# Left output projection with products of 512 columns instead of 256, its even and odd heads summed apart and added by three engines

## The chip, the cores and the metric

The kernel runs on one core of a Trainium2 chip. The metric is the device time of one execution in microseconds (us); a median of several runs is given where there are several. Engines are named as in the profile: PE (TensorE, matmuls), PEld (its weight loads), DVE (VectorE), ACT (ScalarE), POOL (GpSimd) and SP (SyncE, here the queue that streams weights).

## The reference

The input x has 2048 rows of 1024. It is normalised by rows to xn. Part A goes over 64 segments of 32 rows, with a memory of 8 rows that is carried from one segment to the next:

```python
for s in range(n_seg):                      # 64 segments, seg_len 32, M = 8, 32 heads of 128
    h = jnp.concatenate([mem, xs], axis=1)  # 40 rows
    q, k, v = (jnp.einsum('btd,dhe->bhte', h, W) for W in (Wq, Wk, Wv))
    scores = jnp.einsum('bhqe,bhke->bhqk', q, k) * scale
    p = _softmax(jnp.where(mask[None, None], scores, -1000000000.0), axis=-1)
    o = jnp.einsum('bhqk,bhke->bhqe', p, v)
    o = jnp.einsum('bhte,hed->btd', o, Wo)
    mem = o[:, :M, :].copy()
    outs.append(o[:, M:, :])
```

Part B routes: the two rows of xn with the largest product with w_r go through a gated MLP (1024 to 3584 and back), times the sigmoid of that product, and are added to xn there. The output is x + A(xn) + B(xn), in bfloat16.

## The kernel before

**Main rows and left rows.** The first output rows of a segment become the next segment's memory, so the segments run one after another. Of a segment's 32 rows of x, the first 24 (XM) are worked on together with the 8 rows of memory: 32 "main" rows. Its last 8 rows, the "left" rows, depend on no output for their projections, and four segments' left rows are worked on together as one tile of 32 rows. Four segments make a group G; j is the place of a segment in its group (s = 4 G + j). Their attention still needs the segment's keys, so it runs with the segment; its result goes to OTL (32 heads, 4 segments, 8 rows).

**Weights.** The weights of Q, K, V and the output are cut into 64 granules of 128 x 2048. 44 stay in SBUF; 20 are streamed again in each segment by SP through five slots, tile `g`, `fetch()` at L350 (one granule and three quarters of another are kept in PSUM). Granules 48 to 63 are the output's, two heads each.

**Order in a segment.** Six phases p = 0 to 5 (halves of Q, K, V as in `PHASES`), each of eight granules kc: at L785 four products of 32 rows by 512 columns, in four column groups of PE, into `PSm`. At a phase's end ACT copies PSm to SBUF (XB at L804, VM at L814), and PE turns it three granules into the next phase (L621). Scores are formed at (2,6) and (4,6) (L644, L646), DVE and ACT do the softmax (exponential L663, sums L668, last reader of the scores L687), `attend` forms the heads' outputs (L707, L709; copies L716, L718). Phase 6 is the output: 16 granules, each with eight products of 256 columns at L571 (`project`) into `WO`, which DVE adds to the rows of x (L854). The norm and the turns for the next segment run in between.

**Left passes.** The left rows' projections of a group are spread over other segments as passes on granules that are in SBUF at that time. The table `PASSES` names for each unit the place (j, phase, kc) and the granules. The units of Q, K and V run `left_pass` (L564, four products of 512); the unit "o", the output of the previous group's left rows, runs `project` (L571, eight products of 256, from OTL) into `WL`, ten granules at the end of the segment j = 3 and six in the next segment, j = 0. At the place in `COPIES` the unit is copied out: for "o", one addition by DVE (L593) of WL to OL, the left rows of x after `sum_left`, and four stores by POOL (L596). OL is loaded by `load_left` in the segment j = 3. In the last segment all 16 passes "o" follow the main ones.

**Release.** A slot of `g` is loaded anew when PE's last product on it, main or left, has run. After the last segment the routed rows' MLP runs, with its weights loaded into places that have come free.

Of the kernel before, what the change touches and what calls it, by code (L numbers as in the profile page):

```python
# [8 lines left out]
BF16 = mybir.dt.bfloat16  # L9
F32 = mybir.dt.float32  # L10
U32 = mybir.dt.uint32
ALU = mybir.AluOpType
# [31 lines left out]
}  # L44

COPIES = {"q0": (1, 1, 0, "scalar"), "q1": (1, 5, 7, "vector"), "k0": (2, 2, 0, "scalar"), "k1": (3, 1, 0, "scalar"),
          "v0": (3, 4, 7, "scalar"), "v1": (3, 5, 7, "scalar"), "o": (0, 4, 3, "vector")}


@with_exitstack  # L50
def kernel(
# [16 lines left out]
    nc = tc.nc  # L68
    P = 128
    Bsz, S, D = A_x.shape  # L70
    H, E = A_Wq.shape[1], A_Wq.shape[2]
    M = A_mem0.shape[1]
    SEG = int(A_seg_len)
# [9 lines left out]
    XM = SEG - M  # L83
# [34 lines left out]
    one = ctx.enter_context(tc.tile_pool(name="one", bufs=1, reuse_waits="tile"))  # L118
# [78 lines left out]
    for s in range(4):  # L197
        nc.vector.tensor_copy(out=SELM[:, s, :, 0:XM],
                              in_=IDENT[:, 32 * s:32 * s + XM].unsqueeze(1).to_broadcast([P, 4, XM]))
        nc.vector.tensor_copy(out=SELL[:, s, :, :],  # L200
                              in_=IDENT.rearrange("p (s c) -> p s c", c=32)[:, :, XM:SEG])
# [103 lines left out]
    def new_stl(PTl):  # L305
        stl = one.tile([P, KC, SEG], BF16, tag="stl", name="STL")
        nc.scalar.copy(out=gview(stl), in_=PTl[:, :, :, :])
        return stl
# [2 lines left out]
        PTm = turn(OB)  # L311
        nc.vector.tensor_copy(out=gview(st)[:, :, :, XM:SEG], in_=PTm[:, :, :, XM:SEG])

    def load_left(G, t):
        o4 = x2[4 * G * SEG:4 * (G + 1) * SEG, :].rearrange("(s r) d -> s r d", s=4)
        for g in range(4):
            nc.gpsimd.dma_start(out=t[32 * g:32 * (g + 1), :], in_=o4[:, XM:SEG, 256 * g:256 * (g + 1)])
        return t

    def norm_left(t, G):  # L320
# [87 lines left out]
    def granule(g):  # L408
        if g in res_tiles:
            return res_tiles[g]  # L410
        got, t = queued.pop(0)
        assert got == g, (got, g)
        return t
# [107 lines left out]
    def group_of(u, s):  # L521
        G, j = divmod(s, 4)
        if u == "o":
            return G if j == 3 else G - 1
        return G + 1
# [22 lines left out]
    def begin(u):  # L548
        PS = psL.tile([P, 512], F32, tag="accl", name="WL" if u == "o" else "PSl")
        units[u] = [PS, 16 if u == "o" else 8]  # L550

    def one_pass(u, g, Gv):
        if u not in units:
            begin(u)
        PS, n = units[u]
        units[u][1] = n - 1
        if u == "o":
            project(PS, g - 48, Gv, lhs_left, n == 1, first=(n == 16))
        else:
            left_pass(PS, g, Gv, n == 8, n == 1)  # L560

    def left_pass(PSl, g, Gv, first_, last_):
        for jq in range(4):
            nc.tensor.matmul(PSl[32 * jq:32 * jq + 32, :], lhsT=STL[:, g % KC, :], rhs=part(Gv, jq),  # L564
                             start=first_, stop=last_, tile_position=(0, 32 * jq))

    def project(PS, w, Gv, lhs, last, first=False):
        for hs in range(2):
            h = 2 * w + hs
            for g in range(4):  # L570
                nc.tensor.matmul(PS[32 * g:32 * g + 32, 0:256], lhsT=lhs(h),  # L571
                                 rhs=Gv[:, D * hs + 256 * g:D * hs + 256 * (g + 1)], start=(first and hs == 0),
                                 stop=(last and hs == 1), tile_position=(0, 32 * g), skip_group_check=True)

    def lhs_left(h):
        return otl_of[0][:, h, :, :].rearrange("p s r -> p (s r)")

    xl_of, otl_of = [None], [None]

    def copy_unit(u, s, engine):  # L580
        PS, n = units.pop(u)
        assert n == 0, (u, s, n)
        Gu = group_of(u, s)
        copy = nc.scalar.copy if engine == "scalar" else nc.vector.tensor_copy
        half = int(u[-1]) if u != "o" else 0
        if u[0] == "v":
            new_vl[half] = one.tile([P, 512], BF16, tag=roles[half], name="VL")
            copy(out=new_vl[half][:, :], in_=PS[:, :])
            if half:
                roles.insert(0, roles.pop())  # L590
        elif u == "o":
            OL = xl_of[0]
            nc.vector.tensor_tensor(out=OL[:, :], in0=PS[:, 0:256], in1=OL[:, :], op=ALU.add)  # L593
            o4 = out2[4 * Gu * SEG:4 * (Gu + 1) * SEG, :].rearrange("(s r) d -> s r d", s=4)
            for g in range(4):
                nc.gpsimd.dma_start(out=o4[:, XM:SEG, 256 * g:256 * (g + 1)], in_=OL[32 * g:32 * (g + 1), :])  # L596
        else:
            XBl = one.tile([P, 512], BF16, tag=roles[0], name="XBl")
            copy(out=XBl[:, :], in_=PS[:, :])
            stores.append(lambda: nc.scalar.dma_start(out=ql_d[Gu][2 * half + "qk".index(u[0])], in_=XBl[:, :]))  # L600
            if engine == "scalar":
                stores.pop()()

    for s in range(NSEG):
        G, j = divmod(s, 4)
# [89 lines left out]
        def attend(half, ph, turn_too=None):  # L695
            if half not in sums:
                if half not in OT:
                    OT[half] = one.tile([P, 4, 4, SEG], BF16, tag=("kt", "bC")[half], name="OT")
                if half == 0:
                    nxt["wo"] = psA.tile([P, 512], F32, tag="acc", name="WO")  # L700
                sums[half] = [BS[:, 0:4 * NK] if half else nxt["wo"][:, 256:256 + 4 * NK], OPB]
            PTm, PTl = PTs[half]
            for il in range(4):
                for jl in range(2):
                    q0 = 32 * (2 * ph + jl)
                    o = sums[half][jl][:, il * NK:(il + 1) * NK]
                    nc.tensor.matmul(o, lhsT=VM[half][q0:q0 + 32, il * P:(il + 1) * P], rhs=PTm[q0:q0 + 32, il, 0:NK],  # L707
                                     start=True, stop=False, tile_position=(q0, 0), skip_group_check=True)
                    nc.tensor.matmul(o, lhsT=VL[half][q0:q0 + 32, il * P:(il + 1) * P], rhs=PTl[q0:q0 + 32, il, 0:NK],  # L709
                                     start=False, stop=True, tile_position=(q0, 0), skip_group_check=True)  # L710
            if turn_too is not None:
                turn_too()
            for jl in range(2):
                ov = sums[half][jl].rearrange("p (i q) -> p i q", i=4)
                copy = nc.scalar.copy if half == 0 or jl == 0 else nc.vector.tensor_copy
                copy(out=OT[half][:, 2 * ph + jl, :, :], in_=ov[:, :, 0:SEG])  # L716
                h0 = 16 * half + 8 * ph + 4 * jl
                copy(out=left_out()[:, h0:h0 + 4, j, :], in_=ov[:, :, SEG:NK])  # L718
# [58 lines left out]
        for p, (mat, half) in enumerate(PHASES):  # L777
# [3 lines left out]
            for kc in range(KC):  # L781
                g = 8 * p + kc
                Gv = back if s > 0 and g == KEPT_WHOLE else granule(g)
                for jq in range(4):
                    nc.tensor.matmul(PSm[32 * jq:32 * jq + 32, :], lhsT=ST[:, kc, :], rhs=part(Gv, jq),  # L785
                                     start=(kc == 0), stop=(kc == KC - 1), tile_position=(0, 32 * jq))
# [45 lines left out]
        for w in range(16):  # L832
            if w == 5:
                attend(1, 0)
            if w == 8 and s + 1 < NSEG:
                attend(1, 1, lambda: turned.append(turn(xn, BS[:, 160:288].bitcast(BF16))))
                nxt["st"] = new_st(turned[0])
            elif w == 8:
                attend(1, 1)
            if w == 12 and left_too is not None:  # L840
                STL = new_stl(turn(left_too))
            Gv = granule(48 + w)
            project(WO, w, Gv, lhs_main, w == 15, first=(w == 0))
            held[48 + w] = Gv
            run_passes(6, w)
            if w == 9 and s + 1 < NSEG:
                new_lx(s + 1)
                bring_back(1, nc.scalar.copy)
                bring_back(2, nc.vector.tensor_copy)
            if w == 11 and j == 3:  # L850
                xl_of[0] = load_left(G, one.tile([P, 256], BF16, tag="stl", name="OL")[:, :])
            release(6, w)
        OB = X[s % 2]
        nc.vector.tensor_tensor(out=OB[:, :], in0=WO[:, 0:256], in1=OB[:, :], op=ALU.add)  # L854
# [66 lines left out]
    for w in range(2):  # L921
        for kc in range(KC):
            for fh in range(2):
                Gt = moe_tiles["gu", w, kc, fh]
                for fl in range(FC // 2):
                    col = (w * FC + fh * (FC // 2) + fl) * 2
                    nc.tensor.matmul(GU[:, col:col + 2], lhsT=Gt[:, fl * P:(fl + 1) * P], rhs=XSELT[:, kc, :],
                                     start=(w + kc + fh + fl == 0), stop=True, skip_group_check=True)
# [6 lines left out]
    for fg in range(FC // 2):  # L935
        Gt = moe_tiles["dn", fg]
        for a in range(2):
            fc = 2 * fg + a
            for g in range(4):
                nc.tensor.matmul(YP[32 * g:32 * g + 2, 0:256], lhsT=HT[:, fc, :],  # L940
                                 rhs=Gt[:, a * D + 256 * g:a * D + 256 * (g + 1)], start=(fc == 0), stop=(fc == FC - 1),
                                 tile_position=(0, 32 * g))
# [39 lines left out]
```

## Time and profile before

| | |
|---|---|
| median of 3 runs | 1893.31 us (1886.54 to 1896.8) |
| the profiled execution: time, span | 1904.66 us, 1903.0 us |
| mean granted clock of TensorE | 0.955 |
| DMA | 704.02 MB, 370 GB/s in the mean |
| PE matmuls, loads | 36008, 36008 |
| left output products: from resident, from streamed granules | 1408, 640 (128x256) |
| additions at L593 | 16, 390 ns each |

All rows of the prediction come from the profiled execution. In the groups of instructions the columns are: line, engine, operation, output<-input, shape, count, then busy us and mean ns of one, then the idle us of the engine before them and what ended them. "issue" is idle time that ended with nothing that the profile shows. The tables of waits read: who waited for whom, us in total, times, longest.

### The profile page before, as it was taken

What the parts mean: (1) busy time and instruction counts of PE and PEld (TensorE: products, weight loads), DVE (VectorE), ACT (ScalarE), POOL (GpSimd) and SP (SyncE); (2) the same over time, 40 slices, a digit from 0 to 9 for tenths busy, and PEclk for the clock granted to TensorE, in tenths of its full rate; (3) what the DMA queues carried; (4) which work ended last, traced back from release to release, by engine and by line L of the source; (5) the groups of instructions that cost most, each with busy time, mean ns of one, the idle gap of its engine ahead of it and who ended that gap; (6) DMA issues with size and microseconds to landing.
All of it is one profiled execution on the core that took longest, in us unless ns stands there. A gap on an engine that the chain in (4) does not pass through costs nothing.

```text
span 1903.0 us, 82489 instructions
## 1 busy us (share of the span) xinstructions
PE 1583.4 (83%) x36008; PEld 884.0 (46%) x36008; DVE 898.3 (47%) x2970; ACT 683.9 (36%) x1923; POOL 441.6 (23%) x882
## 2 busy tenths in 40 slices
PE   3558888888888988898888988888898898888764
PEld 1224545445454545444454544445444454545443
DVE  5825544544445444544455444544444454445430
ACT  1113433343334433343333333334333343333320
POOL 3211222213131322213121322213132221312220
PEclk9669999999999999999999999999999999999995
DMA  9999999999999999999999999999999999999998
GB/s 359 406 345 377 368 376 371 369 363 367 385 370 380 376 373 375 389 364 352 376 364 379 376 380 367 354 383 361 354 343 379 368 371 377 373 379 352 373 393 330
DMA packets 232090, 704.02 MB, mean 370 GB/s; under 512 B 39296, under 2 KB 61232, under 8 KB 231728
## 3 DMA queue, kind: packets, MB, share of 16 engines
q1 hardware_dynamic: 194384, 662.92, 92.5%
q0 software_dynamic: 28704, 27.96, 4.7%
q10 hardware_dynamic: 8640, 7.87, 1.2%
q8 instruction: 282, 4.62, 0.9%
q14 instruction: 80, 0.66, 0.1%
HBM read 685.93 MB, written 22.16 MB: 372 GB/s over the span
## 4 chain that ended last, share of the span: by engine, by line
DMA 53%; PE 42%; issue 3%; ACT 1%; DVE 1%; SPq 1%; POOL 0%; ACTq 0%; POOLq 0%; DVEq 0%
DMA g<-wsc 45%; PE PSm L785 22%; PE WO L571 6%; PE PSl L564 5%; PE BT L621 3%; PE WL L571 3%; DMA g<-in_A_Wv_dram 1%; DMA MW<-in_B_w_gate_dram 1%; DMA MW<-in_B_w_up_dram 1%; DMA g<-in_A_Wq_dram 1%; PE BS L644 1%; DMA wres<-in_A_Wv_dram 1%; DMA g<-in_A_Wk_dram 1%; DMA wres<-in_A_Wo_dram 1%; DMA g<-in_B_w_down_dram 1%
## 5 line engine op out<-in xcount | busy, mean ns | idle before, releaser
L785 PE MATMUL PSm<-wres,ST 128*32 128x512 bf16 x8448 | 707.7, 385 | 19.6 <-DMA wres<-in_A_Wv_dram 8.3
L785 PEld LDWEIGHTS <-ST 128*32 128x32 bf16 x12288 | 325.7, 96 | 418.5 <-issue 199.9
L785 PE MATMUL PSm<-g,ST 128*32 128x512 bf16 x3588 | 363.8, 388 | 105.7 <-DMA g<-wsc 75.3
L571 PEld LDWEIGHTS <-OT 128*32 128x32 bf16 x8192 | 221.7, 98 | 162.4 <-issue 143.1
L571 PE MATMUL WO<-wres,OT 128*32 128x256 bf16 x5632 | 243.5, 280 | 25.6 <-issue 18.6
L804 ACT CAST XB<-PSm 128x512 bf16<-128x512 f32 x256 | 150.0, 586 | 311.2 <-PE PSm L785 307.8
L480 POOL DMA_DIRECT2D LX<-ql_d x63 | 33.6, 533 | 826.2 <-PE WO L571 399.4
L571 PE MATMUL WO<-g,OT 128*32 128x256 bf16 x2560 | 135.9, 284 | 78.8 <-DMA g<-wsc 67.1
L564 PE MATMUL PSl<-wres,STL 128*32 128x512 bf16 x2112 | 187.4, 395 | 0.8 <-issue 0.7
L856 POOL DMA_DIRECT2D out_dram<-X x256 | 129.4, 513 | 217.3 <-DVE X L854 179.5
L273 POOL DMA_DIRECT2D X<-in_A_x_dram x256 | 129.8, 511 | 183.2 <-PE PSm L785 77.3
L377 DVE COPY g<-BT 128x512 bf16<-128x512 bf16 x63 | 26.7, 425 | 294.4 <-ACT QT L629 224.1
L373 ACT COPY BK<-KEPT 128x512 bf16<-128x512 bf16 x126 | 75.8, 602 | 133.4 <-PE WO L571 133.4
L854 DVE TENSOR_TENSOR X<-WO,X 128x256 bf16<-128x256 f32 x64 | 27.2, 425 | 195.5 <-PE WO L571 195.5
L564 PEld LDWEIGHTS <-STL 128*32 128x32 bf16 x3072 | 85.7, 99 | 59.4 <-issue 14.6
L629 ACT COPY QT<-BT 128x512 bf16<-128x512 bf16 x128 | 74.9, 585 | 106.1 <-PE BT L621 100.8
L621 PEld LDWEIGHTS <-XB 128*128 128x128 bf16 x1024 | 58.7, 98 | 105.8 <-ACT XB L804 58.7
L814 ACT CAST VM<-PSm 128x512 bf16<-128x512 f32 x128 | 75.8, 592 | 85.1 <-PE PSm L785 83.4
L707 PEld LDWEIGHTS <-VM 32*128 32x128 bf16 x2048 | 65.6, 91 | 83.9 <-issue 68.5
L621 PE MATMUL BT<-IDENT,XB 128*128 128x128 bf16 x1024 | 102.6, 223 | 2.3 <-ACT QKL L499 1.4
L653 DVE TENSOR_TENSOR BS<-BS,CT 128x96 f32<-128x96 f32 (+1 forms) x256 | 59.6, 233 | 85.6 <-PE BS L646 81.2
L716 ACT CAST OT<-BS 128x128 bf16<-128x128 f32 x128 | 34.0, 265 | 178.5 <-PE BT L709 85.2
(173 smaller groups left out, 2425.6 us busy)
## 6 DMA issues: line engine op xcount, KB each, us to landing
g<-wsc SPq DMA_DIRECT2D x1134, 512.0 KB, 6.1
LX<-ql_d POOLq DMA_DIRECT2D x63, 128.0 KB, 6.0
g<-wsc SPq DMA_DIRECT2D x63, 128.0 KB, 5.0
ql_d<-XBl ACTq DMA_DIRECT2D x60, 128.0 KB, 5.6
MW<-in_B_w_gate_dram SPq DMA_DIRECT2D x16, 448.0 KB, 9.3
MW<-in_B_w_up_dram SPq DMA_DIRECT2D x16, 448.0 KB, 9.0
wres<-in_A_Wk_dram SPq DMA_DIRECT2D x12, 512.0 KB, 11.8
MW<-in_B_w_down_dram SPq DMA_DIRECT2D x12, 512.0 KB, 10.2
```

The source lines that it names most:

```text
L273: nc.gpsimd.dma_start(out=X[s % 2][32 * g:32 * g + XM, :], in_=x2[s * SEG:s * SEG + XM, 256 * g:256 * (g + 1)])
L373: copy(out=back[c][:, :], in_=KEPT_COLS[KEPT_WHOLE][c])
L564: nc.tensor.matmul(PSl[32 * jq:32 * jq + 32, :], lhsT=STL[:, g % KC, :], rhs=part(Gv, jq), start=first_, stop=last_, tile_position=(0, 32 ...
L571: nc.tensor.matmul(PS[32 * g:32 * g + 32, 0:256], lhsT=lhs(h), rhs=Gv[:, D * hs + 256 * g:D * hs + 256 * (g + 1)], start=(first and hs == ...
L621: nc.tensor.transpose(out=PTq[:, il, :, :].rearrange("p j r -> p (j r)"), in_=XB[:, il * P:(il + 1) * P], identity=IDENT[:, :])
L629: nc.scalar.copy(out=QT[half][:, :, :], in_=pv)
L653: nc.vector.tensor_tensor(out=S4, in0=S4, in1=m, op=ALU.add)
L707: nc.tensor.matmul(o, lhsT=VM[half][q0:q0 + 32, il * P:(il + 1) * P], rhs=PTm[q0:q0 + 32, il, 0:NK], start=True, stop=False, tile_position ...
L785: nc.tensor.matmul(PSm[32 * jq:32 * jq + 32, :], lhsT=ST[:, kc, :], rhs=part(Gv, jq), start=(kc == 0), stop=(kc == KC - 1), tile_position= ...
L804: nc.scalar.copy(out=XB[:, :], in_=PSm[:, :])
L814: nc.scalar.copy(out=VM[half][:, :], in_=PSm[:, :])
L856: nc.gpsimd.dma_start(out=out2[s * SEG:s * SEG + XM, 256 * g:256 * (g + 1)], in_=OB[32 * g:32 * g + XM, :])
```

## The change

A left output pass now has four products of 512 columns: an even head's into rows 0 to 63 of WL (one half of the columns in rows 0 to 31, the other in rows 32 to 63), an odd head's into rows 64 to 127. The sum over the heads thus stands in two places, 64 rows apart, and is put together at the end: ACT copies half of each across the rows to a new tile LF (which takes the buffer of OTL), DVE adds the other half, POOL adds LF to OL. The column blocks of OL lie in another order ("crossed"), in its loads and its stores. The six passes of j = 0 and the sum stand at other places of the segment.

```diff
-          (3, 8, 0): [52, 54], (0, 1, 5): [55], (0, 2, 2): [57], (0, 2, 5): [58], (0, 3, 2): [60], (0, 3, 5): [61],
-          (0, 4, 2): [63]},
+          (3, 8, 0): [52, 54], (0, 0, 7): [55], (0, 1, 3): [57], (0, 1, 7): [58], (0, 2, 3): [60], (0, 2, 6): [61],
+          (0, 3, 2): [63]},
...
-          "v0": (3, 4, 7, "scalar"), "v1": (3, 5, 7, "scalar"), "o": (0, 4, 3, "vector")}
+          "v0": (3, 4, 7, "scalar"), "v1": (3, 5, 7, "scalar"), "o": (0, 3, 3, "vector")}
...
+            b = 2 * (g % 2) + g // 2 if crossed else g
+            nc.gpsimd.dma_start(out=t[32 * g:32 * (g + 1), :], in_=o4[:, XM:SEG, 256 * b:256 * (b + 1)])
...
-            project(PS, g - 48, Gv, lhs_left, n == 1, first=(n == 16))
+            project_left(PS, g - 48, Gv, n == 16, n == 1)
...
+    def project_left(PS, w, Gv, first, last):
+
+        for hs in range(2):
+            lhsT = otl_of[0][:, 2 * w + hs, :, :].rearrange("p s r -> p (s r)")
+            for c in range(2):
+                r0 = 64 * hs + 32 * c
+                nc.tensor.matmul(PS[r0:r0 + 32, :], lhsT=lhsT, rhs=Gv[:, D * hs + 512 * c:D * hs + 512 * (c + 1)],
+                                 start=first, stop=last, tile_position=(0, r0))
...
-            nc.vector.tensor_tensor(out=OL[:, :], in0=PS[:, 0:256], in1=OL[:, :], op=ALU.add)
+            LF = one.tile([P, 256], F32, tag="otl", name="LF")
+            for c in range(2):
+                nc.scalar.copy(out=LF[64 * c:64 * c + 64, :], in_=PS[64 - 64 * c:128 - 64 * c, 256 * c:256 * c + 256])
+            for c in range(2):
+                here = slice(64 * c, 64 * c + 64)
+                nc.vector.tensor_tensor(out=LF[here, :], in0=PS[here, 256 * c:256 * c + 256], in1=LF[here, :], op=ALU.add)
+            nc.gpsimd.tensor_tensor(out=OL[:, :], in0=LF[:, :], in1=OL[:, :], op=ALU.add)
...
+                b = 2 * (g % 2) + g // 2
+                nc.gpsimd.dma_start(out=o4[:, XM:SEG, 256 * b:256 * (b + 1)], in_=OL[32 * g:32 * (g + 1), :])
```

In what the engines are given, three places show it. Before, PE has the pass on granule 55 in phase 1 of a segment j = 0, between granules 13 and 14 (wres_298 is granule 14, wres_1137 granule 55), eight pairs of a load and a product of 256:

```order
L785 LDWEIGHTS ST
L785 MATMUL PSm<-g,ST 32x512
L571 LDWEIGHTS OTL
L571 MATMUL WL<-wres_1137,OTL 32x256
...
L785 LDWEIGHTS ST
L785 MATMUL PSm<-wres_298,ST 32x512
```

Now it stands at the end of phase 0, between granules 7 and 8 (wres_228 and wres_232), as four pairs with 512 columns:

```order
L799 LDWEIGHTS ST
L799 MATMUL PSm<-wres_228,ST 32x512
L584 LDWEIGHTS OTL
L584 MATMUL WL<-wres_1137,OTL 32x512
...
L799 LDWEIGHTS ST
L799 MATMUL PSm<-wres_232,ST 32x512
```

The whole list of PE has 2048 rows fewer. On ACT, phases 2 to 4 of a segment j = 0, before:

```order
L804 CAST XB<-PSm 128x512
L629 COPY QT<-BT 128x512
L663 ACTIVATE BS<-BS 128x320
L804 CAST XB<-PSm 128x512
L634 COPY KT<-QKL 128x16x8
L636 COPY KT<-BT 128x16x32
```

and now:

```order
L818 CAST XB<-PSm 128x512
L643 COPY QT<-BT 128x512
L602 COPY LF<-WL 64x256 x2
L677 ACTIVATE BS<-BS 128x320
L818 CAST XB<-PSm 128x512
L648 COPY KT<-QKL 128x16x8
L650 COPY KT<-BT 128x16x32
```

The two copies to LF stand ahead of the exponential and of the copy XB of phase 3. On DVE at the same place, before:

```order
L659 TENSOR_TENSOR BS<-BS,NM 128x320
L668 TENSOR_REDUCE DN<-BS 128x8
L669 RECIPROCAL DN<-DN 128x8
L675 TENSOR_TENSOR PT_12472<-BS,DN 128x256
L687 TENSOR_TENSOR BX<-BS,DN 128x8x8
L689 STREAM_TRANSPOSE PT_12472<-PT_12472 128x256
L691 STREAM_TRANSPOSE PT_12472<-BX 128x256
L593 TENSOR_TENSOR OL<-WL,OL 128x256
L653 TENSOR_TENSOR BS<-BS,CT 128x4x24
```

and now:

```order
L673 TENSOR_TENSOR BS<-BS,NM 128x320
L605 TENSOR_TENSOR LF<-WL,LF 64x256 x2
L682 TENSOR_REDUCE DN<-BS 128x8
L683 RECIPROCAL DN<-DN 128x8
L689 TENSOR_TENSOR PT_12257<-BS,DN 128x256
L701 TENSOR_TENSOR BX<-BS,DN 128x8x8
L703 STREAM_TRANSPOSE PT_12257<-PT_12257 128x256
L705 STREAM_TRANSPOSE PT_12257<-BX 128x256
L667 TENSOR_TENSOR BS<-BS,CT 128x4x24
```

The addition behind the softmax of the first half has become two, ahead of its sums.

More of the change, by code (lines that the diff above doesn't have):

```diff
@@ L312, in mem_to_st, with load_left @@
         nc.vector.tensor_copy(out=gview(st)[:, :, :, XM:SEG], in_=PTm[:, :, :, XM:SEG])
-    def load_left(G, t):
+    def load_left(G, t, crossed=False):
         o4 = x2[4 * G * SEG:4 * (G + 1) * SEG, :].rearrange("(s r) d -> s r d", s=4)
         for g in range(4):
-            nc.gpsimd.dma_start(out=t[32 * g:32 * (g + 1), :], in_=o4[:, XM:SEG, 256 * g:256 * (g + 1)])
+            b = 2 * (g % 2) + g // 2 if crossed else g
+            nc.gpsimd.dma_start(out=t[32 * g:32 * (g + 1), :], in_=o4[:, XM:SEG, 256 * b:256 * (b + 1)])
         return t
@@ L573, in project @@
                                  stop=(last and hs == 1), tile_position=(0, 32 * g), skip_group_check=True)
-    def lhs_left(h):
-        return otl_of[0][:, h, :, :].rearrange("p s r -> p (s r)")
     xl_of, otl_of = [None], [None]
+    def project_left(PS, w, Gv, first, last):
[5 more added lines that the diff above has]
+                                 start=first, stop=last, tile_position=(0, r0))
     def copy_unit(u, s, engine):
@@ L592, in copy_unit @@
             OL = xl_of[0]
-            nc.vector.tensor_tensor(out=OL[:, :], in0=PS[:, 0:256], in1=OL[:, :], op=ALU.add)
+            LF = one.tile([P, 256], F32, tag="otl", name="LF")
[5 more added lines that the diff above has]
+            nc.gpsimd.tensor_tensor(out=OL[:, :], in0=LF[:, :], in1=OL[:, :], op=ALU.add)
             o4 = out2[4 * Gu * SEG:4 * (Gu + 1) * SEG, :].rearrange("(s r) d -> s r d", s=4)
             for g in range(4):
-                nc.gpsimd.dma_start(out=o4[:, XM:SEG, 256 * g:256 * (g + 1)], in_=OL[32 * g:32 * (g + 1), :])
+                b = 2 * (g % 2) + g // 2
+                nc.gpsimd.dma_start(out=o4[:, XM:SEG, 256 * b:256 * (b + 1)], in_=OL[32 * g:32 * (g + 1), :])
         else:
@@ L850 @@
             if w == 11 and j == 3:
-                xl_of[0] = load_left(G, one.tile([P, 256], BF16, tag="stl", name="OL")[:, :])
+                xl_of[0] = load_left(G, one.tile([P, 256], BF16, tag="stl", name="OL")[:, :], True)
             release(6, w)
```

## The prediction

> **What bounds the kernel now.** I read the page's totals and its chain first, then the table of waits for PE and for the DMA queue, then PE's timeline around the left products, last the segments one against another.
>
> ```profile
> PE 1583.4 (83%) x36008; PEld 884.0 (46%) x36008; DVE 898.3 (47%) x2970; ACT 683.9 (36%) x1923; POOL 441.6 (23%) x882
> q8 instruction: 282, 4.62, 0.9%
> DMA 53%; PE 42%; issue 3%; ACT 1%; DVE 1%; SPq 1%; POOL 0%; ACTq 0%; POOLq 0%; DVEq 0%
> ...
> SPq L350 <- PE PSm L785: 475.2, 651, 5.7
> SPq L350 <- PE WL L571: 59.9, 63, 2.8
> ...
> PE PSm L785 <- DMA g<-wsc: 75.3, 158, 1.7
> PE WO L571 <- DMA g<-wsc: 67.1, 132, 2.1
> PE WO L571 <- issue: 20.8, 21, 2.1
> PE WL L571 <- issue: 11.5, 8, 2.3
> PE PSm L785 <- issue: 9.2, 10, 2.5
> ```
>
> Two things take turns. The weight stream makes PE wait (75.3 + 67.1 us), and the stream itself waits for PE to free one of its five slots (475.2 us behind PSm, 59.9 us behind WL). So a loss on PE is not simply hidden: the ring is often full, and then the transfers stand still with PE. The three last rows are such losses: 20.8 + 11.5 + 9.2 = 41.5 us in 39 waits in which PE waited for no engine and no transfer. One of them, in PE's timeline (start, length, line, count, idle time before):
>
> ```profile
> 1518.16 0.39 PE L571 MATMUL WO<-wres,OT 128*32 128x256 bf16 x8
> 1518.38 0.61 PE L571 MATMUL WL<-wres,OTL 128*32 128x256 bf16 x16
> 1521.33 0.40 PE L571 MATMUL WL<-wres,OTL 128*32 128x256 bf16 x8 [2.34 <-issue]
> ```
>
> PE stops for 2.34 us between two left passes whose operands have long been there. What it lacks is instructions. Row q8 says so first: 282 packets carry 4.62 MB, 16.4 KB each, and PE with its weight loads has 36008 + 36008 = 72016 instructions, so one packet is 255 of them. Second, the count between two such stops: this is every matmul that started between the stop that ended at 1515.12 us and this one (groups of PE in that window, of four rows with x4 the last is shown).
>
> ```profile
> L571 PE MATMUL WO<-wres,OT 128*32 128x256 bf16 x46 | 2.0, 273 | 0.5 <-issue 0.5
> L571 PE MATMUL WO<-g,OT 128*32 128x256 bf16 x24 | 1.2, 274 | 0.0
> L571 PE MATMUL WL<-g,OTL 128*32 128x256 bf16 x24 | 1.2, 273 | 0.0
> L571 PE MATMUL WL<-wres,OTL 128*32 128x256 bf16 x16 | 0.6, 273 | 0.0
> ...
> L709 PE MATMUL BT<-PT,VL 32*128 32x40 bf16 x4 | 0.3, 174 | 0.0
> L293 PE MATMUL BS<-IDENT,XN 128*128 128x128 bf16 x2 | 0.3, 224 | 0.0
> ```
>
> 46 + 24 + 24 + 16 + 4 x 4 + 2 = 128 matmuls, with their loads 256 instructions: the stops lie one block apart. A block that is used up faster than the next one arrives makes PE stop. A pass of 256 columns uses 16 instructions in the time in which a pass of 512 uses 8:
>
> ```profile
> 978.50 0.39 PE L785 MATMUL PSm<-g,ST 128*32 128x512 bf16 x4
> 978.71 0.39 PE L571 MATMUL WL<-wres,OTL 128*32 128x256 bf16 x8
> 978.93 0.82 PE L785 MATMUL PSm<-wres,ST 128*32 128x512 bf16 x12
> ```
>
> From start to start, four products of 512 take 0.21 us and eight of 256 take 0.22 us. What a stop costs is seen in the first segments of the groups (j = 0): seven begin with a stop among the first passes or just behind them, eight don't. The windows' columns are length, then busy time of the engines, clock, DMA share and GB/s; first and last of the seven with their sum, then of the eight.
>
> ```profile
> 431.76:460.13 28.37, 23.20 (x568) 13.57 (x560) 13.80 (x49) 10.57 (x30) 9.91 (x19) 1.00 1.01 371
> 1518.61:1547.55 28.94, 24.02 (x570) 14.54 (x562) 13.70 (x49) 10.44 (x30) 10.34 (x20) 0.94 1.00 367
> sum 202.25, PE 168.91 PEld 98.62 DVE 96.48 ACT 73.43 POOL 70.94; mean PE 24.13 PEld 14.09 DVE 13.78 ACT 10.49 POOL 10.13
> ...
> 214.81:241.74 26.93, 23.18 (x569) 13.64 (x561) 13.79 (x50) 10.56 (x30) 9.65 (x18) 1.00 1.01 371
> 1737.18:1763.40 26.22, 23.20 (x558) 13.65 (x550) 13.22 (x47) 10.05 (x29) 7.31 (x14) 0.98 0.96 344
> sum 213.74, PE 185.74 PEld 108.79 DVE 109.73 ACT 84.10 POOL 75.05; mean PE 23.22 PEld 13.60 DVE 13.72 ACT 10.51 POOL 9.38
> ```
>
> 202.25 / 7 = 28.89 us against 213.74 / 8 = 26.72 us: 2.17 us more. The stops in these seven, read like the one above, last 0.7 to 2.5 us, 1.78 us in the mean, so a stop costs 2.17 / 1.78 = 1.2 times its length. A reason stands in the clock column: it reads 0.94 in five of the seven (as in the last row here) and in one of the eight; after a stop PE runs slower for a while.
>
> **The change part by part.**
>
> *The products.* 256 left passes go from eight to four matmuls: 1024 matmuls and 1024 loads fewer. By the starts above a pass costs 0.21 us instead of 0.22: 256 x 0.01 = at most 2.6 us; I take 0, since that is the rounding of the rows. What counts is the instructions. The block above holds 40 left matmuls; as 20 they leave room for 20 others, so it lasts 20 x 0.22 / 8 = 0.55 us longer, and its stop of 2.34 us is that much shorter. Two other blocks that I counted so, ending in stops of segments 28 and 59, held 30 and 24: mean 31, 0.43 us each. I give this to the 8 waits in WL and to the 13 of the 21 in WO that lie in segments j = 3; the other 8, 4.8 us, lie where few or no left output passes stand in the block: 21 x 0.43 = 9.0 us. The 10 waits in PSm lie mostly in the first half of j = 0, where a block holds about two of the six left passes there: 8 matmuls, 0.22 us, together 2.2 us. Sum 11.2 us of stops, at 1.2 for one 13.4 us. Bounds: nothing, if the packets come later by as much; and 41.5 - 4.8 = 37 us one for one, if every stop near left passes vanishes.
>
> *The moved passes.* Six passes of j = 0 move ahead; by the end of phase 3 six of them are done, before five. One pass (0.22 us) more lies ahead of the phases whose slots the stream waits for: 15 x 0.22 = 3.3 us at most, 0 where PE waits for the stream later anyway. I take 1 us.
>
> *The sums at phase 3, in place of one addition at phase 4.* In segment 32:
>
> ```profile
> 983.89 0.58 ACT L629 COPY QT<-BT 128x512 bf16<-128x512 bf16 x1 [0.87 <-PE BT L621]
> 984.37 0.43 ACT L663 ACTIVATE BS<-BS 128x320 f32<-128x320 f32 x1
> 985.05 0.58 ACT L804 CAST XB<-PSm 128x512 bf16<-128x512 f32 x1 [0.25 <-PE PSm L785]
> 985.94 0.21 DVE L687 TENSOR_TENSOR BX<-BS,DN 128x64 bf16<-128x64 f32 x1
> 986.91 0.39 DVE L593 TENSOR_TENSOR OL<-WL,OL 128x256 bf16<-128x256 f32 x1
> ...
> 986.01 0.40 PE L621 MATMUL BT<-IDENT,XB 128*128 128x128 bf16 x4
> 987.34 0.21 PE L644 MATMUL BS<-KT,QT 128*32 128x40 bf16 x4 [0.17 <-ACT KT L636]
> 989.73 0.40 PE L785 MATMUL PSm<-g,ST 128*32 128x512 bf16 x4 [1.33 <-DMA g<-wsc]
> ...
> L307 ACT COPY STL<-BT 128x256 bf16<-128x256 bf16 x16 | 6.0, 372 | 21.1 <-PE BT L293 21.1
> L731 POOL MEMSET OTL<- 128x256 bf16 x17 | 5.6, 329 | 0.0
> ```
>
> Two ScalarE copies of 256 columns, 0.37 us each by L307, now stand ahead of the exponential. They are done about 0.6 to 0.74 us later than 984.37; the exponential, and behind it the copy XB, slip. XB starts 0.2 to 0.4 us late, so it ends at 985.8 to 986.0 (985.05 + 0.58 before): PE's transposes read it at 986.01. Just covered. On VectorE two additions of 0.39 us (L593) stand ahead of the softmax sums, behind the second copy; the last reader of the scores, L687, goes from 985.94 to about 986.7, and PE writes new scores at 987.34: covered by 0.6 us. The old addition at 986.91 goes. GpSimd's addition isn't in this trace: 0.33 us by its memset, 0.77 us at twice VectorE's row; I take 0.5. Only the four stores behind it and the buffer that LF shares with OTL wait for it, and OTL is written again two phases later. So I cost this at 0; with the cover gone it is up to 0.74 x 15 = 11 us. Even then PE's next wait (1.33 us for the stream at 989.73) takes some of it.
>
> *The end.* The last group's sum gets longer by two copies, one addition and GpSimd's: 0.74 + 0.39 + 0.33 to 0.77 = 1.5 to 1.9 us, ahead of the loads of the routed rows.
>
> ```profile
> 1885.97 10.90 DMA g<-in_B_w_down_dram
> 1896.91 0.62 PE YP L940 x8
> ```
>
> The chain ends on the loads of the last weights, which don't wait for that: 0.
>
> Sum: -13.4 + 1 + 0 = about -12 us. The profiled execution took 1904.66 us (span 1903.0), 11.35 us above the median of 1893.31; 1904.66 - 12 = 1892.7 there, and 1893.31 - 12 = 1881 us for a median run.
>
> **The rivals.**
>
> *The instructions are no limit that this moves.* The Trainium skill, "Runtime: NRT & Kernel Launch", Instruction fetch mechanics, has blocks of 256 instructions that are fetched while the current one runs, a crossing being mostly hidden. Its block agrees with row q8; that crossings are hidden does not agree with 41.5 us in 39 waits. As a mechanism here: the stops come from packets that are late behind the weight stream, and fewer instructions only ask later; or the time won on PE is given back as waits for g<-wsc. For it: PE waits 142.4 us for the stream already. Against it: the 2.17 us. Time: -2.6 to +3.3 us, about 1893.
>
> *Stops vanish.* If the slower use lets most blocks arrive in time, up to 37 us go; half to all of it is 1856 to 1874. Against it: the 2.34 us stop needs more than four times the 0.55 us.
>
> *Slower: ScalarE in front of the K product.* At j = 0, phase 4, the copy XB comes behind two copies and the exponential. From a slip of 0.38 us on (986.01 - 985.63) PE waits for it, at its end for 0.74 us, with the moved pass 0.96 us in each of 15 groups: +14 us, and without the fetch gain 1907. For it: PE already waits for ScalarE there (0.17 us). Against it: the wait for the stream right behind.
>
> **How the numbers follow.** A measurement of this kernel tells about 0.5% (9.5 us) from no change. Chances: forecast 0.5, no limit 0.21, vanish 0.14, slower 0.15. The forecast's own range is -6 to -19 us, from half the gain to one and a half of it; two thirds of it (0.34 of 0.5) lie beyond -9.5 us. Faster: 0.34 + 0.14 = 0.48. Slower: 0.15, all of that rival. Same: 0.16 + 0.21 = 0.37. The range reaches from most of the vanishing case, -29 us, to halfway into the slower one, +7 us: 1864 to 1900.
>
> **What would show it.** Right: WL <- issue falls from 11.5 us to under 7, WO <- issue from 20.8 to under 15, q8 to about 274 packets (2048 instructions less), the first segments of groups from a mean of (202.25 + 213.74) / 15 = 27.7 us to about 27.2. Wrong: these rows unchanged; waits for g<-wsc up by what they lose; waits of PE for XB or KT at phase 4 of j = 0, or of BS <- DVE, above 0.3 us a group.

## Result and the profile after

The changed kernel takes 1889.59 us (median of 22 runs, 1878.39 to 1895.47), the kernel before beside it 1899.35 us (22 runs): a ratio of 0.9942, 95% interval 0.9923 to 0.9962. It is faster by 0.6%, 0.4 to 0.8%. The profiled execution took 1894.10 us (span 1892.5, before 1903.0).

Totals, instruction packets and chain on the page of the changed kernel:

```profile
PE 1577.7 (83%) x34984; PEld 853.2 (45%) x34984; DVE 905.3 (48%) x2986; ACT 694.4 (37%) x1955; POOL 452.7 (24%) x898
q8 instruction: 274, 4.49, 0.9%
DMA 58%; PE 38%; DVE 1%; issue 1%; SPq 1%; ACT 1%; POOL 0%; ACTq 0%; POOLq 0%; DVEq 0%
```

Its table of PE's waits (engine, output, line <- what was waited for: us, times, longest):

```profile
PE PSm L799 <- DMA g<-wsc: 91.2, 168, 2.1
PE WO L572 <- DMA g<-wsc: 64.1, 132, 1.6
...
PE BT L635 <- ACT XB L818: 8.7, 15, 0.8
...
PE WO L572 <- issue: 6.5, 11, 1.2
...
PE PSm L799 <- issue: 3.1, 5, 1.9
...
PE WL L584 <- issue: 2.4, 3, 0.9
```

The three rows of stops fell from 41.5 to 6.5 + 3.1 + 2.4 = 12.0 us. In this profile two rows took most of it back: the waits for the stream rose from 142.4 to 155.3 us, and a wait for the copy XB, which the table of before does not have, lasts 8.7 us, 0.58 us in each of 15 groups. A second profile of the changed kernel (the run beside the products alone, below) has 7.9 us of stops, 8.1 us for XB and only 146.2 us for the stream, so how far the waits for the stream rose is uncertain. All rows of PE's table together went from 300.6 to 295.0 us, 5.6 us less (285.1 in the second profile). PE's busy time fell by as much again, 1583.4 to 1577.7. Most of that fall lies in the 15 first segments of groups, here with their sum (columns as in the prediction):

```profile
215.85:242.86 27.01, 23.09 (x522) 12.42 (x518) 14.23 (x50) 11.33 (x33) 10.34 (x19) 1.00 1.02 385
323.67:349.85 26.18, 23.27 (x522) 12.31 (x518) 14.21 (x50) 11.14 (x33) 10.33 (x19) 1.00 1.02 386
...
sum 409.49, PE 349.92 PEld 187.90 DVE 212.37 ACT 167.71 POOL 154.10; mean PE 23.33 PEld 12.53 DVE 14.16 ACT 11.18 POOL 10.27
```

409.49 / 15 = 27.30 us against 27.7 before; PE is busy there for 349.92 us against 168.91 + 185.74 = 354.65. Most of the time was won elsewhere: counted from one addition to the rows of x (L854, now L868) to the next, the 15 last segments of groups (j = 3), with most left output passes, took 11.8 us less in sum (418.7 to 406.9), the first 6.5 us less, and those between 4.4 us more.

Where the wait for XB comes from, in segment 32 (ScalarE, then PE, by start):

```profile
980.28 0.58 ACT L643 COPY QT<-BT 128x512 bf16<-128x512 bf16 x1 [0.87 <-PE BT L635]
980.87 0.74 ACT L602 COPY LF<-WL 64x256 f32<-64x256 f32 x2
981.52 0.42 ACT L677 ACTIVATE BS<-BS 128x320 f32<-128x320 f32 x1
981.97 0.58 ACT L818 CAST XB<-PSm 128x512 bf16<-128x512 f32 x1
...
982.61 0.40 PE L635 MATMUL BT<-IDENT,XB 128*128 128x128 bf16 x4 [0.57 <-ACT XB L818]
```

The four ScalarE instructions run without a gap, and PE stands for 0.57 us until the last of them is done.

### The profile page after: what moved, and what is told of

The parts are those of the page before. It is cut to its first block, busy times and chain, and to the rows that moved or that the text cites. A ratio compares the mean times of both kernels' runs of the same rounds, so it can differ in the third digit from the quotient of the medians.

```text
span 1892.5 us, 80521 instructions
## 1 busy us (share of the span) xinstructions
PE 1577.7 (83%) x34984; PEld 853.2 (45%) x34984; DVE 905.3 (48%) x2986; ACT 694.4 (37%) x1955; POOL 452.7 (24%) x898
## 4 chain that ended last, share of the span: by engine, by line
DMA 58%; PE 38%; DVE 1%; issue 1%; SPq 1%; ACT 1%; POOL 0%; ACTq 0%; POOLq 0%; DVEq 0%
DMA g<-wsc 49%; PE PSm L799 20%; PE WO L572 5%; PE PSl L565 5%; PE BT L635 3%; PE WL L584 2%; DMA XP<-in_A_x_dram 2%; DMA g<-in_A_Wv_dram 1%; DMA MW<-in_B_w_gate_dram 1%; DMA MW<-in_B_w_up_dram 1%; DMA g<-in_A_Wq_dram 1%; DMA wres<-in_A_Wv_dram 1%; DMA g<-in_A_Wk_dram 1%; DMA wres<-in_A_Wo_dram 1%; SPq L145 1%
## 5 line engine op out<-in xcount | busy, mean ns | idle before, releaser
L572 PEld LDWEIGHTS <-OT 128*32 128x32 bf16 x8192 | 220.2, 98 | 155.3 <-issue 127.7
L868 DVE TENSOR_TENSOR X<-WO,X 128x256 bf16<-128x256 f32 x64 | 27.2, 425 | 177.8 <-PE WO L572 177.8
```

## Experiments

The theory: PE stops because a block of 256 instructions is used up before the next arrives, and the change helps by having fewer instructions. Its rivals: the new places of the passes and of the sum make the difference, not the products; or it is the products' shape and rows, whatever their count of instructions. A question beside these: does PE's wait for ScalarE cost time, or is it given back?

### The products alone, the places alone

The first is the changed kernel with before's places, by this edit; the second is the kernel before with the new places, by the same lines the other way round:

```diff
-          (3, 8, 0): [52, 54], (0, 0, 7): [55], (0, 1, 3): [57], (0, 1, 7): [58], (0, 2, 3): [60], (0, 2, 6): [61],
-          (0, 3, 2): [63]},
+          (3, 8, 0): [52, 54], (0, 1, 5): [55], (0, 2, 2): [57], (0, 2, 5): [58], (0, 3, 2): [60], (0, 3, 5): [61],
+          (0, 4, 2): [63]},
...
-          "v0": (3, 4, 7, "scalar"), "v1": (3, 5, 7, "scalar"), "o": (0, 3, 3, "vector")}
+          "v0": (3, 4, 7, "scalar"), "v1": (3, 5, 7, "scalar"), "o": (0, 4, 3, "vector")}
```

> The changed products and the three-engine sum, at the places of the passes and of the sum before. If the gain comes from fewer instructions on PE: PE's stops without a cause (issue, in front of WO, WL and PSm) fall from 41.5 us to 10 to 16 us as in the changed kernel, and the time is 8 to 13 us under the kernel before. If it comes from the moved passes and the earlier sum: stops fall too, but the time is within 3 us of the kernel before.

> The kernel before with its eight products of 256 columns and its one addition, but the passes of j = 0 and the addition at the new places. Fewer instructions as the cause: 36008 matmuls as before, stops of 35 to 48 us, time within 4 us of the kernel before. The places as the cause: 8 to 12 us faster than before at unchanged stops.

Products alone: 1891.69 us, ratio 0.9974 (0.9948 to 1.0000). That is some 5 us under the kernel before, between the two expectations (8 to 13 us, or within 3), so the time misses both. Places alone: 1902.31 us, 1.0034 (1.0014 to 1.0055), a little over the 4 us expected, so with the old products they cost time by themselves. The stops go with the products: 7.0 + 2.8 + 2.3 = 12.1 us with the products alone, but in PE's waits of the places alone they are 40.0 us, PSm having gained what WO lost:

```profile
PE WO L571 <- issue: 15.0, 16, 2.1
PE PSm L785 <- issue: 13.7, 13, 2.1
PE WL L571 <- issue: 11.3, 10, 1.9
```

So the places are not where the gain comes from. Yet the products alone gain only half of what the whole change does. The next run, on one chip with the changed kernel once more, was to show whether this is real.

> The changed kernel itself, on the same chip as the next three, so that they can be set against it: 9 to 13 us under the kernel before, stops (issue) in front of WO, WL and PSm 10 to 16 us.

> Once more the changed products and sum at the places of before, beside the changed kernel. If the places matter with the new products, it is 4 to 8 us slower than the changed kernel, its waits for g<-wsc or its first segments of groups longer; if not, within 3 us of it.

Changed kernel: 1884.79 us, 0.9952 (0.9935 to 0.9969), with 7.9 us of stops, fewer than the 10 to 16 expected; products alone: 1892.41 us, 0.9972 (0.9950 to 0.9994); the means are 6.2 us apart, with a standard error of 1.6, so it is. In PE's waits with the products alone (here the first of their two runs) one row has grown:

```profile
PE WO L721 <- ACT OTL L732: 14.6, 15, 1.5
```

In the kernel before PE waited there 1.8 us in all. With the sum left at phase 4 the wait is not for XB but for OTL at phase 5. In sum it is no longer (14.6 and 11.4 us in the two runs, where XB and OTL together take 11.2 and 11.6 us in the two profiles of the changed kernel); a single wait is, up to 1.5 us against 0.8. What else differs is PE's busy time, 1586.0 and 1586.6 us against 1577.7 and 1577.0, and the granted clock, which reads 0.94 or less in 8 and 11 of the 15 first segments against 2 and 3. How much of the 6.2 us is the wait and how much the clock these runs don't separate; the light stream below shows both again. So the places don't bring the gain; they lower the price of the longer sum.

### The same products cut into 256 and 128 columns

Everything else of the changed kernel stays: places, rows, copies, sum. The edit for 256 columns; for 128 the range is 4 and the step 128.

```diff
-            for c in range(2):
-                r0 = 64 * hs + 32 * c
-                nc.tensor.matmul(PS[r0:r0 + 32, :], lhsT=lhsT, rhs=Gv[:, D * hs + 512 * c:D * hs + 512 * (c + 1)],
-                                 start=first, stop=last, tile_position=(0, r0))
+            for i in range(2):
+                for c in range(2):
+                    r0 = 64 * hs + 32 * c
+                    col = D * hs + 512 * c + 256 * i
+                    nc.tensor.matmul(PS[r0:r0 + 32, 256 * i:256 * (i + 1)], lhsT=lhsT, rhs=Gv[:, col:col + 256],
+                                     start=(first and i == 0), stop=last, tile_position=(0, r0), skip_group_check=True)
```

> The changed kernel with each left product of 512 columns cut into two of 256: layout, sums, places and streamed columns as in the changed kernel, the number of instructions as before (36008 matmuls, 282 packets). Instructions as the cause: stops go back to 35 to 50 us and the time to that of the kernel before, from 2 us under it to 6 us over it. Anything else as the cause: it stays 8 to 12 us under the kernel before.

> The changed kernel with each left product of 512 columns cut into four of 128: 16 matmuls and 16 loads a pass, 2048 matmuls more than the kernel before would have with 8 (38056 in all, about 298 packets), the same streamed columns. If instructions are what PE lacks: stops grow to 75 to 110 us and the time to 15 to 35 us over the kernel before. If a pass's columns or its places set the time: like the cut to 256, 4 to 10 us over the kernel before.

Cut to 256: 1905.47 us, ratio 1.0043 (1.0022 to 1.0064); PE's stops and the packets:

```profile
PE WO L572 <- issue: 22.6, 18, 3.0
PE WL L586 <- issue: 10.4, 9, 2.3
...
PE PSm L801 <- issue: 6.5, 6, 1.6
```

```profile
q8 instruction: 282, 4.62, 0.9%
```

Cut to 128: 1951.57 us, 1.0318 (1.0286 to 1.0351):

```profile
PE WO L572 <- issue: 28.7, 19, 3.0
PE PSm L801 <- issue: 21.5, 11, 4.0
PE WL L586 <- issue: 21.5, 13, 3.4
```

```profile
q8 instruction: 298, 4.88, 1.0%
```

With 4, 8 and 16 matmuls a pass the stops are 12.0, 39.5 and 71.7 us, the packets 274, 282 and 298, the ratios to the kernel before, each on its own chip, 0.994, 1.004 and 1.032. Both cuts cost more than expected: 7.5 us over the kernel before where 6 was the bound, and 56.6 where 35 was, the latter with stops a little under the 75 us expected. The 256 cut brings nearly all stops back at the new places, in the new rows and with the new sum, so neither of these is what took them away. The ratios also split the change: as many instructions as before, with all else of the change, cost 0.4%; fewer instructions bring that back and 0.6% more. In the last step the ratio grew by 0.0275, some 52 us, for 32 us more stops. PE's busy time also grew (368.11 us in the first segments of groups, against 353.90 when cut to 256), and the granted clock reads 0.97 or less in 11 of these 15 segments, against 2. So not all of it is the instructions' coming; whether the stops or the narrower products lowered the clock is not shown.

### The sum one phase later

```diff
-          "v0": (3, 4, 7, "scalar"), "v1": (3, 5, 7, "scalar"), "o": (0, 3, 3, "vector")}
+          "v0": (3, 4, 7, "scalar"), "v1": (3, 5, 7, "scalar"), "o": (0, 4, 0, "vector")}
```

> The changed kernel with the sum at phase 4, granule 0, behind the copy XB of phase 3 on ScalarE. PE's waits for XB in front of its turns (8.7 us in 15 waits in the changed kernel) fall under 2 us. If these waits lie on the path the time is 4 to 8 us under the changed kernel; if the wait for the weight stream behind them takes them up, it is within 3 us of the changed kernel (that is 8 to 14 us under the kernel before).

Measured 1886.43 us, ratio 0.9949 (0.9924 to 0.9974), the changed kernel's own within the interval. The row of XB is gone from PE's waits. The waits for the stream, 152.9 us, lie between the 155.3 and the 146.2 of the changed kernel's two profiles, so they don't show by themselves where the 8.7 us went:

```profile
PE PSm L799 <- DMA g<-wsc: 82.7, 188, 1.7
PE WO L572 <- DMA g<-wsc: 70.2, 146, 1.7
```

So the 8.7 us that PE waits for XB are worth nothing that these runs can tell while the stream is this full.

### A lighter stream

If packets are late behind the weight stream, they come in time when the stream is light; and with PE as the bound the price of the sum must show. From the second segment on a streamed granule is here 512 columns instead of 2048, and PE reads these in place of the others, so the projections on streamed granules are other numbers; the count and shape of PE's instructions are the same.

```diff
-        return slice(0, 512 if s > 0 and g == KEPT_PART else 2048)
+        return slice(0, 512 if s > 0 else 2048)
...
+    def cols(t, a, n):
+        a = a % 512 if id(t) in small else a
+        return t[:, a:a + n]
```

It was made of the kernel before, of the changed one, of that with the sum at (0, 4, 0), and of the products alone.

> The kernel before with a quarter of the weight stream: from the second segment on each streamed granule is loaded with its first 512 columns alone, and PE reads those 512 columns in place of the others (the result is another one). PE's instructions are the same in number and order. If the packets of instructions are late because they stand behind the weight stream, the stops fall under 10 us although PE runs denser (segments of about 21 to 24 us). If PE itself can't take in instructions faster, the stops stay at 40 us or grow.

> The changed kernel with the same quarter of the weight stream as in the run before it (streamed granules' first 512 columns alone, PE reads them in place of the others; the result is another one). No stops were left there, so what is seen is the change without its effect on stops. If fewer instructions help only through the stops: not faster than the kernel before with the light stream (1651.5 us), but 2 to 9 us slower, by the waits for XB (8 us in 14 waits with the whole stream). If halving the instructions also shortens PE's own work: 3 us or more faster than 1651.5 us.

> The same with the sum at phase 4, granule 0, as in the run with the sum later. Where PE is the bound, a wait for XB isn't given back: this should be 4 to 9 us faster than the light run with the sum at phase 3, its waits for XB gone, and within 2 us of 1651.5 us. If it is no faster, these waits cost nothing even there.

> The light-stream kernel with the wide products (a streamed granule is a quarter from segment 1 on, PE reads that quarter in place of the rest), but with the six passes of j = 0 and the sum back at their places of before. If the 5.7 us left with the later sum come from the moved passes (in segment 32 the wait for KT at phase 4 is 0.31 us against 0.17, the one for OTL 0.78 against 0.56, together 0.36 us a group), they go here: j = 0 back to 23.46 us, 1651.5 us within 2. If they come from the products of 512 or from the three engines' longer sum, they stay: 1655 to 1659 us, j = 0 at 23.8.

| with the light stream | us (4 runs each) | first segments of groups, sum of 15 |
|---|---|---|
| before | 1651.46 (1650.99 to 1653.56) | 350.90 |
| changed | 1664.15 (1663.24 to 1664.60) | 362.96 |
| changed, sum at (0, 4, 0) | 1657.20 (1655.84 to 1658.83) | 356.63 |
| products alone | 1677.14 (1676.78 to 1677.65) | 376.87 |

The runs come from three chips: before from one, the two changed ones from a second, the products alone from a third. With the full stream the kernel before has medians of 1895.0, 1891.4 and 1898.1 us on them, so small differences are read from the segments, not from the totals.

Totals and packets of the kernel before, now with the light stream:

```profile
PE 1502.8 (91%) x36008; PEld 869.8 (53%) x36008; DVE 893.0 (54%) x2970; ACT 676.3 (41%) x1923; POOL 439.5 (27%) x882
q8 instruction: 282, 4.62, 1.2%
```

The same 36008 matmuls in the same 282 packets, used 15% faster (1903.0 / 1649.4), and yet the table of PE's waits has only one row of stops left, 4.6 us in the MLP at the end; PSm, WO and WL have none. So PE's pace alone doesn't make the stops: the packets were late because of the full stream. The profile has no landing times of the instruction packets, but it has those of transfers that are the same in both runs, here one of 128 KB, first with the full stream, then with the light one (the last number is the median from issue to landing, in us):

```profile
LX<-ql_d POOLq DMA_DIRECT2D x63, 128.0 KB, 6.0
```

```profile
LX<-ql_d POOLq DMA_DIRECT2D x63, 128.0 KB, 2.9
```

The loads of x, 12 KB each and so nearer to a packet's 16.4 KB, took 5.0 and 2.3 us. Between the two stops read in the prediction PE used up its 256 instructions in 6.21 - 2.34 = 3.87 us (from the end of the first stop, 1515.12, to the end of the second, 1521.33, less the second). That a packet takes as long as such a load is an estimate; by it, it comes later than the block lasts with the full stream, and earlier with the light one.

Without stops to save, the change is a loss of 12.7 us, 0.8%, more than expected, and nearly all of it lies in the first segments of groups (362.96 - 350.90 = 12.1 us). PE's waits of the changed kernel with the light stream:

```profile
PE WO L729 <- ACT OTL L740: 20.8, 33, 0.7
...
PE BT L643 <- ACT XB L826: 8.8, 15, 0.8
```

8.8 us for XB, and 2.4 us more for OTL than the 18.4 us of before. Putting the sum later takes away 7.0 us, as expected of it, but leaves 5.7 where at most 2 were expected: in segment 32 PE waits for KT at phase 4 for 0.31 us (before 0.17), and for OTL for 0.78 us (before 0.56). Over the run these two rows are 4.8 against 2.5 us and 22.0 against 18.4, together 5.9 us more, which is the whole remainder.

I took the moved passes for the cause of these 5.7 us, and the products alone were to show it by returning to 1651.5 us. They took 1677.14: a miss for both sides of that expectation, and the largest price of all. VectorE in its segment 32, then PE:

```profile
868.79 0.45 DVE L713 STREAM_TRANSPOSE PT<-BX 128x256 bf16<-128x256 bf16 x1
870.34 0.86 DVE L613 TENSOR_TENSOR LF<-WL,LF 64x256 f32<-64x256 f32 x2 [1.10 <-ACT LF L610]
871.23 0.27 DVE L675 TENSOR_TENSOR BS<-BS,CT 128x96 f32<-128x96 f32 x1
...
873.85 0.17 PE L729 MATMUL WO<-PT,VM 32*128 32x40 bf16 x1 [1.71 <-ACT OTL L740]
```

The additions wait 1.10 us for ScalarE's copies, the mask of the second half's scores (L675) stands behind them on VectorE, and with it slip the exponential, the softmax and OTL: PE waits 1.71 us where it was 0.56 before (over the run 35.7 us against 18.4). The first segments cost 26.0 us more than before, 1.73 us each, with 1.15 us more of this wait. PE's busy time in them grew too, by 15.1 us in sum (346.82 against 331.75): in 14 of the 15 the granted clock reads 0.93, where it was 1.00 in all 15 before (the first two are shown). In the other segments of the groups, j = 1 to 3, it reads 1.00 in both runs, so the lower clock belongs to these segments and not to the chip.

```profile
188.18:212.76 24.58, 22.16 (x522) 12.51 (x518) 14.24 (x51) 11.18 (x33) 10.62 (x20) 1.00 0.44 122
283.22:308.31 25.09, 23.16 (x522) 13.05 (x518) 14.36 (x50) 11.24 (x33) 10.59 (x20) 0.93 0.42 114
```

So the sum over three engines needs an earlier place, and the last pass of the group (before at phase 4, kc 2) has to move ahead of it. What is left of the 5.7 us, moved passes or the sum at (0, 4, 0), these runs don't separate.

## Why the prediction was right, and where two errors cancelled

*The cause* was right, and is shown: stops follow the count of instructions (4, 8, 16 matmuls a pass) at one layout and place, and vanish with a light stream. The signs announced came: WL 11.5 to 2.4 us, WO 20.8 to 6.5, q8 at 274, first segments 27.7 to 27.3. One announced sign of being wrong came as well, a wait for XB of over 0.3 us a group (see the sum below). The rival "no limit" falls with its time of about 1893 us without a change. But its reason for the stops, packets that are late behind the weight stream, is what the light stream shows; and that time won is given back as waits for g<-wsc may hold for a part, 12.9 us in the profile after and 3.8 in the second one.

*The stops* were mis-sized. I let each shorten by as much as its block lasts longer, 21 x 0.43 + 2.2 = 11.2 us; they fell by 29.5, near the 37 us that I had kept as the bound. For the stops it is thus the rival "stops vanish" (chance 0.14, half to all of 37 us) that came, though not its time of 1856 to 1874 us. Against the 256 cut, 8 packets more mean 27.5 us more stops. Why half a microsecond more in a block takes more than that off the stops is not shown by these runs.

*The price of a stop* was mis-sized the other way. I counted 1.2 us for one, read from first segments with a stop against those without. 29.5 us of stops less, with 8.7 us of new waits, brought the profiled execution 10.5 us. Against the 256 cut, where all else is the same, 27.5 us of stops are worth 1.0% of the time, 19 us: 0.7 us for one. The price depends on the place. In the last segments of groups, 13.6 us of stops fewer than with the cut to 256 go with 14.2 us less time; in the first segments, from which I took the price, 11.1 us fewer go with only 4.1 us less. The comparison was also less clean than I wrote: seven of the eight segments that I took as free of an early stop hold stops too, all but one of them 0.8 to 1.4 us in sum; the mean of the eight is 0.78 us a segment, that of the seven 2.40. And the clock is no mark of a stop: it reads 0.94 or less in 2 of 15 first segments when cut to 256, with 39.5 us of stops, and in 8 of 15 with the products alone, with 12.1. Why a stop costs less in the first segments is not shown. That the stream, where it is behind, makes PE wait at the next granule instead would fit.

*The moved passes* were costed at +1 us, 3.3 at most. With the old products the new places, of the passes and of the addition, cost 0.3% (0.1 to 0.6%, that is 3 to 10 us); with the new ones they bring 6.2. Neither is in the forecast's term, and what makes the old products slower there is not shown.

*The sum at 0* is half right. The copy XB was not "just covered": PE waits 0.58 us in every group. I had kept its turns at 2.12 us behind the start of the copy QT (983.89 to 986.01). In the changed kernel PE was ready at 982.61 - 0.57 = 982.04, 1.76 us behind that start (980.28), since two left passes (on granules 61 and 63) had stood between them and were moved ahead. I had put one of them into the slower rival (0.96 us) and left both out of the forecast. The copy XB itself began 1.69 us behind QT's start instead of 1.16, so it slipped by 0.53 us and not by 0.2 to 0.4. What the wait costs is another matter: nothing that can be told with the full stream (sum later, 1886.43 us), 7.0 us with the light one. The slower rival had the mechanism and not the price: it let PE's waits become the end's, while with the full stream they cost nothing that the runs can tell.

*GpSimd's addition* lies within its bounds of 0.33 to 0.77 us, above the 0.5 taken. The view by tile, LF (duration in ns, least, median and most):

```profile
L602 ACT COPY LF<-WL x32: 363/366/368, 227.4 to 1833.2; 64x256 f32<-64x256 f32 x32
L605 DVE TENSOR_TENSOR LF<-WL,LF x32: 408/422/428, 228.1 to 1834.3; 64x256 f32<-64x256 f32 x32
L606 POOL TENSOR_TENSOR OL<-LF,OL x16: 661/664/686, 229.1 to 1835.3; 128x256 bf16<-128x256 f32 x16
```

*The products' own time* was rightly taken as 0: with the light stream the last segments of groups, with most left passes, take 24.5 us in both kernels, and the whole difference lies in the first ones.

*The end* was rightly taken as 0: in the chain that ended last, the MLP's weights begin at 1838.86 us before and at 1828.36 now, and both kernels end 64 us behind that.

*The time*: -12 us was forecast, -10.5 in the profiles and -9.8 between the medians came. The 1881 us stood on a median of three runs; on that of 22, 1899.35, the same -12 gives 1887, against 1889.59 measured. Too small a fall of the stops and too high a price for each cancelled, which is luck; the time alone would not have told.

## What to carry to other kernels

Where PE stops with all operands there, count the matmuls between two such stops and set the count against the instruction packets: if stops are one packet apart, fewer and wider products are worth time that no busy row shows. Then ask what makes the packets late; here it was the weight stream, and with a quarter of it the same change loses 0.8%. Before a pass is moved, see which wait it covered, and on which engine's queue a new sum stands ahead of something that PE needs.

## What the runs showed of the hardware

- Stops for instructions depend on what else the DMA engines carry: 41.5 us at 370 GB/s, none in the projections at 123 to 131 GB/s, though PE used its instructions 15% faster. Loads of 12 KB took 5.0 us from issue to landing in the first case and 2.3 us in the second. The Trainium skill, "Runtime: NRT & Kernel Launch", Instruction fetch mechanics, has the crossing of a block as mostly hidden; that agrees with the light stream's runs and not with the full stream's.
- 1024 matmuls and as many loads more, in the same work on the same columns, cost 1.0% of this kernel's time (ratios 0.994 and 1.004), with 27.5 us more of stops and 3.6 us more of PE's busy time (1581.3 against 1577.7).
- With the light stream, a wait of 1.71 us instead of 0.56 in the first segment of each group came with a granted clock of 0.93 instead of 1.00 in 14 of 15 of them, and with 1.73 us more time a segment for 1.15 us more of the wait.
